# Turning double-precision weights into float32 on two engines, and spreading the recurrent units evenly, in an mLSTM + MLP kernel

## The chip, the cores and the metric

The kernel runs on one core of one Trainium2 chip. The metric is the device time of one execution in microseconds (us); lower is better. The engines of the core are named as in the profile: PE (TensorE, the matrix engine; PEld is its weight load), DVE (VectorE), ACT (ScalarE), POOL (GpSimd) and SP, whose queue issues nearly all DMAs.

## The reference

A recurrence over 768 positions for 4 x 8 heads of width 40 (an mLSTM with stabilised exponential gates), and behind it a two-layer MLP on its output, 3072 rows of 320, with a hidden width of 2048:

```python
for t in range(S):                       # per batch b and head h
    m_new = np.maximum(f_gate[:, :, t] + m, i_gate[:, :, t])
    f_stab = np.exp(f_gate[:, :, t] + m - m_new)
    i_stab = np.exp(i_gate[:, :, t] - m_new)
    C = f_stab * C + i_stab * outer(v_t, k_t)
    n = f_stab * n + i_stab * k_t
    y[:, :, t] = sigmoid(o_t) * (C @ q_t) / np.maximum(np.abs(n . q_t), 1.0)
x = y as (3072, 320)
h = x @ w_in                             # w_in  320 x 2048
out = (h * sigmoid(h)) @ w_out           # w_out 2048 x 320
```

The two weight matrices arrive as float64 (10.5 MB together); everything else is float32.

## The kernel before

**Units and steps.** The recurrence is cut into 12 chunks of 64 positions, and the batch into 2 pairs: 24 units of 128 output rows. Three units make a step, so there are 8 steps. For each step the MLP runs over 16 column blocks `fc` of the hidden width: `mm1(fc)` makes a 128 x 384 block `ph` (8 matmuls, weights and activations split in a high and a low part), ACT takes its tanh `th`, DVE makes the gated value `g` (step 0) or its high and low parts `gh`, `gl`, and `mm2(fc - 2)` adds that block's share to the three output tiles `pout`. In PE's order an `mm1` therefore alternates with an `mm2` two blocks behind. `ph` has two PSUM buffers, `pout` three, so the first `mm2` of a step waits until ACT has copied the step before it out of `pout` (tiles `ob`).

**Pieces.** The units of the *next* step are computed between the blocks of the running one. `piece` cuts a unit into five pieces. Piece 0 issues the loads of unit n+2, the scores of unit n+1 (`ps`), the values of unit n (`po`) and its state (`pu`): its front on PE. DVE then runs the chain `nq`, `den`, `x` that ends in the copy of line 433. Piece 1 transposes `x` on PE (`px`) into the step's activations `xh`, `xl`. Pieces 2 and 3 are gate activations and decays (`ko`, `lq`, `D`, on ACT and POOL). `SCHED` gives the unit reached at each step's start; the pieces of a step are spaced evenly between its two numbers, by the `while done < ...` loop. The numbers come to 3.2, 5, 3.4, 2.4, 2.4, 2.8 and 1.8 units in the seven steps.

**Weights.** The doubles come in 18 parts, each with one buffer `wr` out of ten: 8 parts of `w_in` (`i0` to `i7`, 512 doubles a partition, two column blocks each), 8 of `w_out` (`o0` to `o7`, 640 doubles) and two for the last 64 rows of `w_in` (`c0`, `c4`). `Part.make` turns the two 32-bit words of each double (`low`, `high`) into a float32 in `wt` (or `wo`), and then splits that into a high part (ACT copy, lines 224, 234 and 244) and a low part (DVE subtraction, lines 225, 235, 245). After each part the load of the next is issued. Five parts are made before step 0, the rest in step 0's blocks 0 to 5, by the digits of `FILL`.

**Order.** SP and, in the step loop, PE run in the order in which the code is written. DVE, ACT and POOL run in an order that the scheduler fixes when the program is built; each engine then executes its own list strictly in that order. A DVE instruction of a unit can thus stand behind weight instructions that have nothing to do with it.

Of the kernel before, what the change touches and what calls it, by code (L numbers as in the profile page):

```python
# [8 lines left out]
F32 = mybir.dt.float32  # L9
F32R = mybir.dt.float32r  # L10
U32 = mybir.dt.uint32
AF = mybir.ActivationFunctionType
ALU = mybir.AluOpType
PSUM = bass.MemoryType.PSUM
# [6 lines left out]
NU = NC * NP  # L21
# [3 lines left out]
UPS = 3  # L25
# [8 lines left out]
NBIG = 10  # L34
NWT = 3
PRI = 20
SCHED = [3, 6.2, 11.2, 14.6, 17.0, 19.4, 22.2, 24]
FILL = "2114231113212412"

TINY = 2.0**-15  # L40


@with_exitstack
def mlstm_mlp_kernel(
# [11 lines left out]
    nc = tc.nc  # L56
# [5 lines left out]
    pw = pool("pw", NWT)  # L62
# [15 lines left out]
        out=tri, in_=tri, compare_op=ALU.is_ge, fill=NEG, base=0,  # L78
# [10 lines left out]
    pq = pool("pq", DFF // 256)  # L89
    wo, wol = {}, {}  # L90
# [73 lines left out]
    WN = max(2 * WC, 2 * DM)  # L164
    wide = w_in.dtype != F32

    class Part:
# [7 lines left out]
        def load(self):  # L175
            K, nb, n, nm = self.K, self.nb, self.n, self.nm
            if wide:
                t = pb.tile([128, WN, 2], U32, tag="big", name=f"wr{nm}")[:, : nb * n, :]
                self.raw = t.rearrange("p (a f) w -> p a f w", a=nb)
                to, src = t.rearrange("p (a f) w -> p a (f w)", a=nb), self.src.bitcast(U32)  # L180
            else:
# [11 lines left out]
        def make(self):  # L193
            K, nb, n, nm = self.K, self.nb, self.n, self.nm
            full = self.raw
            if wide:


                low, high = full[:, :, :, 0], full[:, :, :, 1]
                bits = pw.tile([128, WN], U32, tag="wt", name=f"wt{nm}")  # L200
                bits = bits[:, : nb * n].rearrange("p (a f) -> p a f", a=nb)
                mag = full = bits.bitcast(F32)
                nc.scalar.activation(mag, high.bitcast(F32), AF.Abs)
                nc.vector.tensor_scalar(mag, mag, TINY, None, op0=ALU.max)
                nc.vector.tensor_scalar(
                    bits, bits, 3, 0x3FFFFFF8, op0=ALU.logical_shift_left, op1=ALU.bitwise_and
                )
                nc.vector.scalar_tensor_tensor(
                    out=bits, in0=high, scalar=0xC0000000, in1=bits,
                    op0=ALU.bitwise_and, op1=ALU.bitwise_or,  # L210
                )
                if self.i is not None:
                    full = wo[self.i] = pq.tile([128, nb, n], F32, tag="wo", name=f"w{nm}")
                nc.vector.scalar_tensor_tensor(  # L214
                    out=full.bitcast(U32), in0=low, scalar=29, in1=bits,
                    op0=ALU.logical_shift_right, op1=ALU.bitwise_or,
                )
            elif self.i is not None:
                wo[self.i] = pq.tile([128, nb, n], F32, tag="wo", name=f"w{nm}")
                nc.vector.tensor_copy(wo[self.i], full)  # L220
            if self.i is not None:
                return
            if K == 128:
                nc.scalar.copy(self.hi, full)
                nc.vector.tensor_tensor(
                    out=self.lo, in0=full, in1=self.hi.bitcast(F32), op=ALU.subtract
                )
            else:

                for k in range(2):  # L230
                    a, b = slice(k * K, (k + 1) * K), slice((1 - k) * K, (2 - k) * K)
                    cs = slice(k * n, (k + 1) * n)
                    hi = self.hi[a, :, cs]
                    nc.scalar.copy(hi, full[a])
                    nc.vector.tensor_tensor(
                        out=self.hi[b, :, cs], in0=full[a], in1=hi.bitcast(F32), op=ALU.subtract
                    )

    def split_out(i):

        full, hi = wo.pop(i), woh[:, 2 * i : 2 * i + 2, :]
        to, tag = (pq, "wo") if i else (pw, "wt")
        wol[i] = to.tile([128, 2, DM], F32R, tag=tag, name=f"wol{i}")
        nc.scalar.copy(hi, full)
        nc.vector.tensor_tensor(out=wol[i], in0=full, in1=hi.bitcast(F32), op=ALU.subtract)
# [25 lines left out]
    def wmake(n):  # L271

        for p in parts[nmade[0] : nmade[0] + n]:
            p.make()
            wload(1)
        nmade[0] = min(nmade[0] + n, len(parts))
# [16 lines left out]
    class Unit:  # L293
# [62 lines left out]
        def decay(self):  # L356
            nc.gpsimd.tensor_tensor(out=self.Dm, in0=self.Dm, in1=self.am, op=ALU.add)  # L357
            nc.scalar.activation(self.Dm, self.Dm, AF.Exp)

        def misc(self):  # L360
            nc.scalar.activation(self.ot, self.ot, AF.Tanh, scale=0.5)
            if self.c > 0:
                nc.scalar.activation(self.lq, self.lq, AF.Exp)  # L363
                self.qt = p2.tile([KS, H, L], F32, tag="qt", name=f"qt{self.n}")
                nc.gpsimd.tensor_tensor(out=self.qt, in0=self.q, in1=self.lq, op=ALU.mult)  # L365
# [109 lines left out]
    class Step:  # L475
# [10 lines left out]
        def mm1(self, fc):  # L486
# [14 lines left out]
            with tc.high_priority(offset=PRI):  # L501

                th = p2.tile([128, NT], F32, tag="th", name=f"th{j}_{fc}")
                nc.scalar.activation(th, ph, AF.Tanh, scale=0.5)  # L504
                if j == 0:
# [44 lines left out]
        def store(self, t):  # L550
# [4 lines left out]
            else:  # L555
                ob = pb.tile([128, DM], F32, tag="big", name=f"ob{n}")
            nc.scalar.activation(ob, self.po[t], AF.Copy, scale=0.5)  # L557
            for k in range(2):
# [4 lines left out]
    units = [Unit(n) for n in range(NU)]  # L563
    steps = {}

    def piece(i):

        n, k = divmod(i, 5)
        u = units[n]
        if k == 0:  # L570
            if n + 2 < NU:
                units[n + 2].load()
            if n + 1 < NU:
                units[n + 1].scores()
            u.values()
            u.state()
        elif k == 1:
            if n + 2 < NU:
                units[n + 2].shift()
            if n % UPS == 0:  # L580
                steps[n // UPS] = Step(n // UPS)
            u.xpose(steps[n // UPS])
        elif k == 2:
            if n + 1 < NU:
                units[n + 1].misc()
        elif k == 3:
            if n + 2 < NU:
                units[n + 2].decay()
# [57 lines left out]


    ctx.enter_context(tc.manual_schedule(engines={mybir.EngineType.PE}))
    done = 5 * UPS
    for j in range(NSTEP):  # L650
        st = steps[j]
        for fc in range(NFC):
            st.mm1(fc)
            wmake(int(FILL[fc]) if j == 0 else 2)
            if j == 1 and fc % 2 == 0:
                split_out(fc // 2)
            want = 5 * NU
            if j < NSTEP - 1:
                want = 5 * (SCHED[j] + (SCHED[j + 1] - SCHED[j]) * min(fc + 1, 15) / 15)
            while done < min(want, 5 * NU):  # L660
                piece(done)
                done += 1
            if fc >= LAG:
                st.mm2(fc - LAG)
            elif j > 0:
                steps[j - 1].mm2(NFC - LAG + fc)
# [71 lines left out]
```

## Time and profile before

| what | value |
|---|---|
| time, median of 3 runs | 543.53 us (539.04 to 546.12) |
| the profiled execution's own time | 542.31 us |
| its span in the trace | 540.4 us |
| PE busy / DVE busy / ACT busy / POOL busy | 446.9 / 331.6 / 196.6 / 133.2 us |
| mean granted TensorE clock | 0.94 |
| DMA moved | 48.5 MB |

The span is what the trace covers, from the first to the last instruction of the program; the 1.9 us between it and the profiled execution's own time lie around it. Busy times are sums over the whole span, which has two very different stretches: weights and first units up to about 150 us, the steady MLP after it. `L214` is line 214 of the kernel. In a row of the timeline stand start, duration, engine, line, operation, output<-inputs, and in brackets the idle time of the engine before it with what ended it.

### The profile page before, as it was taken

The numbers are of one execution on the slowest core, as the hardware profiler recorded it, in microseconds if no ns is written. First come the engines' busy times: TensorE is split into PE (matmuls) and PEld (weight loads), VectorE is DVE, ScalarE is ACT, GpSimd is POOL, SyncE is SP. The second block draws the span as 40 slices with busy tenths as digits, with TensorE's granted clock in tenths as the row PEclk, the third lists the DMA queues.
The fourth block names the chain that finished last, engine by engine and source line by source line (L and its number), as shares of the span: only waits on it lengthen the run. The fifth ranks groups of instructions, "written<-read, shape, count | busy, mean of one in ns | idle before, by whom it ended". The sixth has DMA issues, their size and how long they took to land.

```text
span 540.4 us, 10327 instructions
## 1 busy us (share of the span) xinstructions
PE 446.9 (83%) x4068; PEld 417.7 (77%) x4068; DVE 331.6 (61%) x669; ACT 196.6 (36%) x397; POOL 133.2 (25%) x129
## 2 busy tenths in 40 slices
PE   1532419269998998899999999899999999999995
PEld 0431318257888898898899998889989999999995
DVE  7999997945356676556656555366556453544441
ACT  1333334311243333533353243333534333334332
POOL 4644511502225443244124122141122000000000
PEclk9966658779999999999999999899999999999999
DMA  5999662512144334443124123230332001001001
GB/s 126 274 297 238 178 230 89 117 37 58 47 123 123 105 105 121 124 106 105 44 81 123 50 56 92 51 103 15 93 94 65 2 1 36 1 1 37 1 1 36
DMA packets 28163, 48.47 MB, mean 90 GB/s; under 512 B 4340, under 2 KB 15060, under 8 KB 28116
## 3 DMA queue, kind: packets, MB, share of 16 engines
q1 hardware_dynamic: 24228, 43.79, 29.7%
q10 hardware_dynamic: 3888, 4.03, 3.1%
q8 instruction: 32, 0.52, 0.4%
q14 instruction: 15, 0.12, 0.1%
HBM read 43.78 MB, written 4.03 MB: 88 GB/s over the span
## 4 chain that ended last, share of the span: by engine, by line
issue 29%; PE 23%; DMA 19%; DVE 13%; POOL 9%; SPq 4%; ACT 3%; ACTq 1%; POOLq 0%; DVEq 0%
PE ph L500 11%; PE pout L540 10%; DMA ko<-in_ko_dram 5%; DMA lq<-LFd 5%; POOL Cm L456 4%; DMA D<-LFd 4%; POOL D L357 3%; POOL am L349 2%; DMA qk<-in_qk_dram 2%; SPq L338 2%; DMA wri<-in_w_in_dram 1%; DVE wo L214 1%; SPq L304 1%; DVE D L393 1%; DVE Cm L462 1%
## 5 line engine op out<-in xcount | busy, mean ns | idle before, releaser
L500 PE MATMUL ph<-xh,wh 128*128 128x384 f32 x384 | 135.5, 353 | 1.0 <-ACT xh L470 1.0
L500 PE MATMUL ph<-xl,wh 128*128 128x384 f32 x384 | 132.1, 344 | 0.6 <-DVE xl L471 0.6
L513 DVE SCALAR_TENSOR_TENSOR th<-th,ph 128x384 f32<-128x384 f32 x112 | 61.9, 553 | 101.7 <-ACT th L504 101.7
L519 DVE TENSOR_TENSOR gl<-th,gh 128x384 fp32r<-128x384 f32 x112 | 77.2, 690 | 63.2 <-ACT gh L518 61.4
L540 PE MATMUL pout<-woh,gh 128*128 128x320 f32 x336 | 107.9, 321 | 5.6 <-ACT ob L557 5.3
L540 PE MATMUL pout<-woh,gl 128*128 128x320 f32 x336 | 104.0, 310 | 0.0
L540 PE MATMUL pout<-wol,gh 128*128 128x320 f32 x336 | 103.8, 309 | 0.0
L504 ACT ACTIVATE th<-ph 128x384 f32<-128x384 f32 x128 | 62.4, 487 | 98.9 <-PE ph L500 97.6
L500 PE MATMUL ph<-xh,wl 128*128 128x384 f32 x256 | 87.7, 343 | 0.0
L456 POOL TENSOR_TENSOR Cm<-Cm,lq 40x328 f32<-40x328 f32 x40 | 33.9, 847 | 176.1 <-PE po L408 158.0
L500 PEld LDWEIGHTS ph<-xh,wh 128*128 128x128 f32 x384 | 73.8, 192 | 2.6 <-ACT xh L470 1.3
L518 ACT CAST gh<-th 128x384 fp32r<-128x384 f32 x112 | 57.2, 511 | 50.2 <-DVE th L513 49.5
L500 PEld LDWEIGHTS ph<-xl,wh 128*128 128x128 f32 x384 | 73.7, 192 | 2.3 <-DVE xl L471 1.0
L540 PEld LDWEIGHTS pout<-woh,gh 128*128 128x128 f32 x336 | 63.2, 188 | 9.8 <-ACT ob L557 7.4
L540 PEld LDWEIGHTS pout<-woh,gl 128*128 128x128 f32 x336 | 63.3, 188 | 0.3 <-DVE gl L519 0.3
L540 PEld LDWEIGHTS pout<-wol,gh 128*128 128x128 f32 x336 | 63.3, 188 | 0.0
L468 PE MATMUL px<-ident,x 128*128 128x128 f32 x72 | 14.5, 307 | 50.7 <-DVE x L430 48.4
L468 PEld LDWEIGHTS px<-ident,x 128*128 128x128 f32 x72 | 8.6, 151 | 56.7 <-issue 33.4
L365 POOL TENSOR_TENSOR qt<-qk,lq 104x512 f32<-104x512 f32 x22 | 30.2, 1371 | 89.9 <-ACT lq L363 70.7
L500 PEld LDWEIGHTS ph<-xh,wl 128*128 128x128 f32 x256 | 49.2, 192 | 0.0
L363 ACT ACTIVATE lq<-lq 104x512 f32<-104x512 f32 x22 | 13.9, 630 | 79.6 <-DMA lq<-LFd 79.6
L357 POOL TENSOR_TENSOR D<-D,am 128x512 f32<-128x512 f32 x24 | 34.6, 1444 | 10.7 <-DMA D<-LFd 10.0
(74 smaller groups left out, 515.8 us busy)
## 6 DMA issues: line engine op xcount, KB each, us to landing
qk<-in_qk_dram SPq DMA_DIRECT2D x24, 416.0 KB
ko<-in_ko_dram SPq DMA_DIRECT2D x24, 320.0 KB
D<-LFd SPq DMA_DIRECT2D x48, 128.0 KB
wro<-in_w_out_dram SPq DMA_DIRECT2D x8, 640.0 KB
wri<-in_w_in_dram SPq DMA_DIRECT2D x8, 512.0 KB
vb<-in_vp_dram SPq DMA_DIRECT2D x48, 82.0 KB
out_dram<-ob ACTq DMA_DIRECT2D x48, 80.0 KB
lq<-LFd SPq DMA_DIRECT2D x22, 128.0 KB
```

Of the source, the lines that this page charges most:

```text
L338: nc.sync.dma_start(to[r], lf[k].unsqueeze(0).broadcast_to([w, 2, 4 * L]))
L357: nc.gpsimd.tensor_tensor(out=self.Dm, in0=self.Dm, in1=self.am, op=ALU.add)
L363: nc.scalar.activation(self.lq, self.lq, AF.Exp)
L365: nc.gpsimd.tensor_tensor(out=self.qt, in0=self.q, in1=self.lq, op=ALU.mult)
L456: nc.gpsimd.tensor_tensor(out=v, in0=v, in1=self.lq[r, :, L - 1].unsqueeze(2).broadcast_to([D, H, D1]), op=ALU.mult,)
L468: nc.tensor.transpose(px[:, c, :], self.x[:, c, :], ident)
L500: nc.tensor.matmul(ph, w, x, start=(i == 0), stop=(i == len(ops) - 1))
L504: nc.scalar.activation(th, ph, AF.Tanh, scale=0.5)
L513: nc.vector.scalar_tensor_tensor(out=th, in0=th, scalar=1.0, in1=ph, op0=ALU.add, op1=ALU.mult)
L518: nc.scalar.copy(gh, th)
L519: nc.vector.tensor_tensor(out=gl, in0=th, in1=gh.bitcast(F32), op=ALU.subtract)
L540: nc.tensor.matmul(self.po[t], g[:, ts], w, start=(fc == 0 and i == 0), stop=(last and i == len(ops) - 1),)
```

## The change

In `Part.make` five operations on each part become three. Before: ACT takes the magnitude of the high word (line 203); DVE clamps it (204), shifts and masks it (205), merges the sign (208), and merges the low word's top bits (214). Now ACT rescales the high word in place (`Prelu` with a tiny scale; its `alpha` serves the negative numbers), ACT turns the top byte of the low word into the three bits that are wanted, in place too, and one DVE operation shifts and merges both. In place means in `wr`, where the words of a double lie 8 bytes apart. A `w_out` part now goes to `wo` without passing `wt`.

The placing of units changes: `PLACES` gives, for step 0 and for all others, the block at which each of the next step's three units starts, and its pieces follow in the next blocks, one for each.

```diff
-SCHED = [3, 6.2, 11.2, 14.6, 17.0, 19.4, 22.2, 24]
+PLACES = ((3, 7, 11), (2, 7, 12))
...
-                bits = pw.tile([128, WN], U32, tag="wt", name=f"wt{nm}")
-                bits = bits[:, : nb * n].rearrange("p (a f) -> p a f", a=nb)
-                mag = full = bits.bitcast(F32)
-                nc.scalar.activation(mag, high.bitcast(F32), AF.Abs)
-                nc.vector.tensor_scalar(mag, mag, TINY, None, op0=ALU.max)
-                nc.vector.tensor_scalar(
-                    bits, bits, 3, 0x3FFFFFF8, op0=ALU.logical_shift_left, op1=ALU.bitwise_and
+                if self.i is not None:
+                    bits = pq.tile([128, nb, n], F32, tag="wo", name=f"w{nm}")
+                    wo[self.i] = bits
+                else:
+                    bits = pw.tile([128, WN], F32, tag="wt", name=f"wt{nm}")
+                    bits = bits[:, : nb * n].rearrange("p (a f) -> p a f", a=nb)
+                h32 = high.bitcast(F32)
+                nc.scalar.activation(h32, h32, AF.Prelu, scale=2.0**-112, alpha=-(2.0**32))
+                nc.scalar.activation(low, full.bitcast(U8)[:, :, :, 3], AF.Copy, scale=1 / 32, bias=-31 / 64)
+                nc.vector.scalar_tensor_tensor(
+                    out=bits.bitcast(U32), in0=high, scalar=3, in1=low,
+                    op0=ALU.logical_shift_left, op1=ALU.bitwise_or,
                 )
-                nc.vector.scalar_tensor_tensor(
-                    out=bits, in0=high, scalar=0xC0000000, in1=bits,
-                    op0=ALU.bitwise_and, op1=ALU.bitwise_or,
-                )
-                if self.i is not None:
-                    full = wo[self.i] = pq.tile([128, nb, n], F32, tag="wo", name=f"w{nm}")
-                nc.vector.scalar_tensor_tensor(
-                    out=full.bitcast(U32), in0=low, scalar=29, in1=bits,
-                    op0=ALU.logical_shift_right, op1=ALU.bitwise_or,
-                )
+                full = bits
...
             if j < NSTEP - 1:
-                want = 5 * (SCHED[j] + (SCHED[j + 1] - SCHED[j]) * min(fc + 1, 15) / 15)
-            while done < min(want, 5 * NU):
-                piece(done)
-                done += 1
+                for u, at in enumerate(PLACES[min(j, 1)]):
+                    if 0 <= fc - at < 4:
+                        piece((j + 1) * UPS + u, fc - at)
```

Three places of the engines' lists show what moves. In the rows stand the line, the operation, output<-inputs and the shape; the first number in a name is that of the unit, part or step (`wri7` is the raw buffer of part `i7`, `th0_4` the tanh of step 0, block 4), the number behind the underscore is that of the buffer.

The first place is SP's queue of loads in the middle of the weights, behind the loads of unit 4. Before:

```order
L186 DMA wri4_554<-in_w_in_dram 128x2x512
L186 DMA wro4_563<-in_w_out_dram 128x2x640
L304 DMA D5_565<-LFd_108 64x512 x2
L312 DMA qk5_568<-in_qk_dram 104x1024
L319 DMA ko5_570<-in_ko_dram 128x640
L325 DMA vb2_116<-in_vp_dram 64x328 x2
L338 DMA lq5_574<-LFd_108 64x2x256
L338 DMA lq5_574<-LFd_108 40x2x256
L186 DMA wri5_670<-in_w_in_dram 128x2x512
```

Now:

```order
L184 DMA wri4_540<-in_w_in_dram 128x2x512
L184 DMA wro4_546<-in_w_out_dram 128x2x640
L184 DMA wri5_567<-in_w_in_dram 128x2x512
L184 DMA wro5_586<-in_w_out_dram 128x2x640
L184 DMA wri6_615<-in_w_in_dram 128x2x512
L184 DMA wro6_623<-in_w_out_dram 128x2x640
L184 DMA wri7_629<-in_w_in_dram 128x2x512
L184 DMA wro7_637<-in_w_out_dram 128x2x640
L298 DMA D5_639<-LFd_108 64x512 x2
```

The loads of unit 5 moved from before part `i5` to behind all weights, because unit 3, whose piece 0 issues them, now starts at block 3 of step 0 and not at block 0.

The second place is ACT's list in the middle of step 0. Before, between the tanh of block 4 and that of block 5:

```order
L504 ACTIVATE th0_4_772<-ph0_4_763 128x384
L203 ACTIVATE wto6_881<-wro6_739 128x640
L203 ACTIVATE wti7_888<-wri7_748 128x512
L244 CAST woh_98<-wo5_781 128x640
L224 CAST wh_96<-wti6_783 128x2x256
L358 ACTIVATE D6_791<-D6_791 128x512
L361 ACTIVATE ko6_796<-ko6_796 128x320
L363 ACTIVATE lq6_800<-lq6_800 104x512
L203 ACTIVATE wto7_896<-wro7_758 128x640
L504 ACTIVATE th0_5_877<-ph0_5_868 128x384
```

Now, ahead of the tanh of block 4:

```order
L238 CAST woh_98<-wo4_625 128x640
L205 ACTIVATE wro5_586<-wro5_586 128x640
L206 ACTIVATE wro5_586<-wro5_586 128x640
L218 CAST wh_96<-wti5_631 128x2x256
L205 ACTIVATE wri6_615<-wri6_615 128x512
L206 ACTIVATE wri6_615<-wri6_615 128x512
L205 ACTIVATE wro6_623<-wro6_623 128x640
L206 ACTIVATE wro6_623<-wro6_623 128x640
L238 CAST woh_98<-wo5_729 128x640
L205 ACTIVATE wri7_629<-wri7_629 128x512
L206 ACTIVATE wri7_629<-wri7_629 128x512
L498 ACTIVATE th0_4_725<-ph0_4_716 128x384
```

Each part stands twice in ACT's list, and the conversion of `i7` stands one block earlier against the tanh values. One table load stands in ACT's whole list, as before.

The third place is DVE's list at the chain of a unit that PE transposes in the middle of step 0. Before, the end of unit 4's chain (its transposition stands in PE's list behind `mm1` of block 5):

```order
L422 RECIPROCAL den4_842<-den4_842 128x8
L225 TENSOR_TENSOR wl_97<-wti7_888,wh_96 128x2x256
L208 SCALAR_TENSOR_TENSOR wto7_896<-wro7_758,wto7_896 128x640
L427 TENSOR_TENSOR x4_848<-po4_825,den4_842 128x320
L214 SCALAR_TENSOR_TENSOR wo7_901<-wro7_758,wto7_896 128x640
L245 TENSOR_TENSOR wol1_1327<-wo1_493,woh_98 128x640
L430 SCALAR_TENSOR_TENSOR x4_848<-ko4_498,x4_848 128x320
L433 COPY x4_848<-x4_848 128x64
```

Now, the end of unit 3's chain (its transposition stands behind `mm1` of block 4):

```order
L416 RECIPROCAL den3_690<-den3_690 128x8
L219 TENSOR_TENSOR wl_97<-wti5_631,wh_96 128x2x256
L207 SCALAR_TENSOR_TENSOR wti6_733<-wri6_615 128x512
L421 TENSOR_TENSOR x3_696<-po3_673,den3_690 128x320
L207 SCALAR_TENSOR_TENSOR wo6_765<-wro6_623 128x640
L424 SCALAR_TENSOR_TENSOR x3_696<-ko3_445,x3_696 128x320
L207 SCALAR_TENSOR_TENSOR wti7_769<-wri7_629 128x512
L239 TENSOR_TENSOR wol0_1140<-wo0_358,woh_98 128x640
L427 COPY x3_696<-x3_696 128x64
```

The unit that is caught among the conversions is now unit 3 and not unit 4, and the last conversion ahead of its copy is that of `i7`. Over the whole program DVE has 54 instructions less and ACT 18 more. In PE's list of steps 1 to 6, pieces 0 now stand behind `mm1` of blocks 2, 7 and 12 and the transpositions behind `mm1` of blocks 3, 8 and 13. Before, steps 2 to 6 had an `mm1` of block 2 directly followed by the first `mm2` of the step; now a piece 0 stands between the two.

More of the change, by code (lines that the diff above doesn't have):

```diff
@@ L11 @@
 U32 = mybir.dt.uint32
+U8 = mybir.dt.uint8
 AF = mybir.ActivationFunctionType
@@ L36 @@
 PRI = 20
-SCHED = [3, 6.2, 11.2, 14.6, 17.0, 19.4, 22.2, 24]
+PLACES = ((3, 7, 11), (2, 7, 12))
 FILL = "2114231113212412"
-TINY = 2.0**-15
 @with_exitstack
@@ L564, in mlstm_mlp_kernel, with piece @@
     steps = {}
-    def piece(i):
-        n, k = divmod(i, 5)
+    def piece(n, k):
         u = units[n]
@@ L648, in mlstm_mlp_kernel @@
     ctx.enter_context(tc.manual_schedule(engines={mybir.EngineType.PE}))
-    done = 5 * UPS
     for j in range(NSTEP):
@@ L656, in mlstm_mlp_kernel @@
                 split_out(fc // 2)
-            want = 5 * NU
             if j < NSTEP - 1:
-                want = 5 * (SCHED[j] + (SCHED[j + 1] - SCHED[j]) * min(fc + 1, 15) / 15)
-            while done < min(want, 5 * NU):
-                piece(done)
-                done += 1
+                for u, at in enumerate(PLACES[min(j, 1)]):
+                    if 0 <= fc - at < 4:
+                        piece((j + 1) * UPS + u, fc - at)
             if fc >= LAG:
```

## The prediction

> **What bounds the kernel now.** I read the busy slices first, then the same in windows, then what PE waited for. Two slice rows of the page, each slice 13.5 us:
>
> ```profile
> PE   1532419269998998899999999899999999999995
> DVE  7999997945356676556656555366556453544441
> ```
>
> DVE is full for the first seven slices and PE is not; from the ninth it is the other way round. The windows (length, busy time and number of instructions of each engine, granted clock, DMA share, GB/s) fix the places:
>
> ```profile
> core 0: us, PE busy (x) PEld busy (x) DVE busy (x) ACT busy (x) POOL busy (x), PEclk, DMA share, GB/s
> 20.00:40.00 20.00, 10.51 (x153) 9.12 (x155) 19.79 (x42) 8.17 (x14) 9.76 (x8) 0.76 1.00 303
> 40.00:60.00 20.00, 4.66 (x71) 3.22 (x67) 19.81 (x37) 7.72 (x15) 7.62 (x5) 0.59 1.01 254
> 60.00:65.00 5.00, 4.40 (x48) 3.50 (x50) 5.00 (x6) 2.58 (x6) 3.52 (x3) 0.55 0.53 132
> 80.00:98.00 18.00, 17.00 (x140) 14.98 (x141) 13.42 (x25) 7.92 (x14) 4.44 (x4) 0.86 0.43 115
> 98.00:112.00 14.00, 0.46 (x3) 0.14 (x1) 13.90 (x24) 4.75 (x8) 3.85 (x3) 0.64 0.24 56
> 112.00:152.00 40.00, 38.92 (x310) 32.24 (x311) 18.89 (x42) 7.53 (x16) 6.51 (x7) 0.95 0.21 57
> ```
>
> In these stretches up to 112 us DVE is 99% busy, but for 80 to 98 (75%); ACT is at 34 to 52%, and DMA is full only until about 62 us. The list of waits and PE's timeline name the wait that ends last there:
>
> ```profile
> PE px L468 <- DVE x L430: 48.4, 18, 13.9
> PEld pout L540 <- ACT ob L557: 7.4, 7, 2.4
> ...
> 57.20 0.66 PE L468 MATMUL px<-ident,x 128*128 128x128 f32 x2 [12.02 <-DVE x L430]
> 112.39 0.88 PE L468 MATMUL px<-ident,x 128*128 128x128 f32 x3 [13.94 <-DVE x L430]
> 115.73 0.58 PE L500 MATMUL ph<-xh,wh 128*128 128x384 f32 x1
> 152.45 0.58 PE L500 MATMUL ph<-xh,wh 128*128 128x384 f32 x1
> ```
>
> PE stood 13.94 us before unit 4's transposition, because its `x` on DVE stood among weight conversions. From there to step 1 (152.45) PE is full: 40.1 us. After that the span is PE's, 540.4 - 152.45 = 387.9 us with the tail. Unit 2's transposition, the last before step 0, had waited 12.02 in the same way. So the change can win before 112 us on DVE, and later only in PE's small waits.
>
> **What the edit of the weights removes.** Three views by line, the whole span, busy us and number of instructions (lines 204, 205, 208), then ACT's groups (count, busy us, mean ns):
>
> ```profile
> 0.00:541.00 541.00, 10.50 (x18) 0.94 0.33 90
> 0.00:541.00 541.00, 13.03 (x18) 0.94 0.33 90
> 0.00:541.00 541.00, 16.01 (x18) 0.94 0.33 90
> ...
> L203 ACT ACTIVATE wto<-wro 128x640 f32<-128x640 f32 x8 | 6.3, 783 | 2.1 <-DMA wro<-in_w_out_dram 2.1
> L203 ACT ACTIVATE wti<-wri 128x512 f32<-128x512 f32 x8 | 5.4, 671 | 1.8 <-DMA wri<-in_w_in_dram 1.8
> L244 ACT CAST woh<-wo 128x640 fp32r<-128x640 f32 x8 | 5.8, 721 | 17.6 <-DVE wo L214 17.6
> L224 ACT CAST wh<-wti 128x512 fp32r<-128x512 f32 x8 | 4.9, 617 | 9.8 <-DVE wti L214 9.8
> L504 ACT ACTIVATE th<-ph 128x384 f32<-128x384 f32 x128 | 62.4, 487 | 98.9 <-PE ph L500 97.6
> L214 DVE SCALAR_TENSOR_TENSOR wti<-wri,wti 128x512 uint32<-128x512 uint32 x8 | 5.4, 680 | 0.0
> L214 DVE SCALAR_TENSOR_TENSOR wo<-wro,wto 128x640 uint32<-128x640 uint32 x8 | 9.5, 1189 | 0.0
> ```
>
> DVE loses 10.5 + 13.0 + 16.0 = 39.5 us, 2.2 us a part, all before 112 us. Line 214 is replaced by one operation of the same kind; no row has both inputs 8 bytes apart. I take 0.68 and 0.82 us (what line 214 takes when nothing disturbs it); the upper end is the row's 1.19 us. ACT gains 18 operations, and all 36 work in place, which no row shows. From below they cost a plain copy, 0.62 and 0.72 us; from above I take POOL's 1.44 us for a 128x512 tile, the slowest elementwise row near. The nearest row is line 203, which reads the same words: 0.67 and 0.78 us. I take that.
>
> The writes 8 bytes apart have a rule in the Trainium skill, "SBUF — State Buffer", the note on cachelines: lines are 16 bytes, and two hits in each suffice for full bandwidth. Words 8 bytes apart hit each line twice, so by it the in-place operations cost nothing extra. For reads the trace agrees (671 ns against 617 for contiguous data); no run here shows the writes.
>
> **What is late next: ACT's list and DMA.** With DVE relieved, unit 3 is the one whose chain stands among conversions; its copy stands behind part `i7`, whose two ACT operations stand at the end of an unbroken row of conversions. When can they be done? DMA rows of SP's queue, and one load on the chain that ended last:
>
> ```profile
> 49.00 1.18 SPq L338 DMA_DIRECT2D lq<-LFd  x2
> 57.88 1.12 SPq L325 DMA_DIRECT2D vb<-in_vp_dram  x2
> 68.36 1.21 SPq L338 DMA_DIRECT2D lq<-LFd  x2
> 77.16 0.37 SPq L186 DMA_DIRECT2D wri<-in_w_in_dram  x1
> ...
> 26.64 4.31 DMA lq<-LFd
> ```
>
> Before, SP sat from 59.0 (57.88 + 1.12) to 68.36 on unit 5's `lq` load (its buffer was held by unit 3), and `i7` was issued only at 77.16. That load now stands behind the weights. DMA was full to about 62.6 us (0.53 of the window 60 to 65), with unit 5's D, qk, ko and vb in it: 256 + 416 + 320 + 164 KB, 4.7 us at 254 GB/s. Without them everything to `o4` is in at 58, and `i5`, `o5`, `i6`, `o6`, `i7` (3 x 512 + 2 x 640 KB, 2.9 MB) take 11.4 us more: `i7` lands at **69**.
>
> ACT: unit 4's `lq` was issued at 49.0 to 50.2; with the 4.3 us of an `lq` load, and something more in a full queue, it lands near 56. Behind it, up to `i7`'s second operation, stand 8 in-place operations of 512 (5.4 us), 6 of 640 (4.7), one `lq` exponential (0.63), three tanh (1.5), four casts of `wh` (2.5) and two of `woh` (1.4): 16.1 us, so 72.1, later than DMA. Then DVE: merge 0.68, one `wol` 0.83, the copy 0.2, and some 1.2 us of hand-overs: unit 3's transposition at **75 us**. Is PE there by then? Unit 2's transposition was at 57.2; seven parts ahead of it at 2.2 us less would give 42. DMA is as full as before, so I take 48. Five `mm1`, two `mm2` and a front, two of the blocks at half clock, are some 16 us by the prices below: PE is done at 64, stands 11 us, and its clock falls as before.
>
> The Trainium skill, "ScalarE: Activation LUTs", speaks against the move: its "Rules for kernel authors" put multiplications on VectorE, as faster. Here the rows are even (671 ns on ACT, 680 on DVE), and what counts is the list that is shorter. By the formula in "What ACT_TABLE_LOAD costs" (186 ns + 0.833 ns an element) the 14 operations are an estimated 9.2 us, not 10.1; the transposition would come 0.9 us earlier.
>
> **From there to step 1.** Prices of PE, from starts of `mm1` in step 0, then in step 3:
>
> ```profile
> 124.77 0.57 PE L500 MATMUL ph<-xh,wh 128*128 128x384 f32 x1
> 130.45 0.58 PE L500 MATMUL ph<-xh,wh 128*128 128x384 f32 x1
> 134.68 0.58 PE L500 MATMUL ph<-xh,wh 128*128 128x384 f32 x1
> 149.44 0.58 PE L500 MATMUL ph<-xh,wh 128*128 128x384 f32 x1
> ...
> 278.08 0.34 PE L500 MATMUL ph<-xh,wh 128*128 128x384 f32 x1
> 280.80 0.34 PE L500 MATMUL ph<-xh,wh 128*128 128x384 f32 x1
> 286.21 0.33 PE L500 MATMUL ph<-xh,wh 128*128 128x384 f32 x1
> 288.56 0.52 PE L468 MATMUL px<-ident,x 128*128 128x128 f32 x3 [0.79 <-DVE x L430]
> 290.23 0.33 PE L500 MATMUL ph<-xh,wh 128*128 128x384 f32 x1
> 486.90 0.34 PE L500 MATMUL ph<-xh,wh 128*128 128x384 f32 x1
> ```
>
> Step 0: a block 3.01 (149.44 to 152.45), with a front 5.68, with a transposition 4.23. From unit 3's transposition remain: its block at half clock, 3.34 (112.39 to 115.73); blocks 5 to 15, 11 x 3.01 = 33.1; two fronts, 2 x 2.67; two transpositions, 2 x 1.22. That is 44.2: step 1 at 75 + 44.2 = **119.2**.
>
> **The even spread.** Later a block takes 2.72 (278.08 to 280.80), with a front 5.41 (+2.69), with a transposition that waits 0.79 for DVE 4.02 (+1.30). Six steps of three units: 6 x (43.5 + 8.1 + 3.9) = 333.0. The last step and tail stay: 540.4 - 486.9 = 53.5. I take 3 off because units 22 and 23 have no state and less scores and `Cm` work. Sum 383.5, against 387.9 before, although unit 6's front (2.7) moves in from step 0 and every transposition now waits 0.79 (before, five units had it across a step's end and did not). What pays is the 7.4 us of waits on `ob`: each step from 1 to 6 now has a front between block 2 and the first `mm2`, which covers them, as in steps 1 and 3 before; one remains. The bounds: without that cover the waits come back, 7 us more; less than the sum it cannot be by much, since steps 1 to 6 are then PE's own time and its 0.79.
>
> Span 119.2 + 383.5 = 502.7, with 1.9 around it 504.6; the profiled execution (542.31) lay 1.2 under the median, so **506 us**.
>
> **Rivals.**
> - PE is not held at all: ACT overlaps its operations and all lands early, the transposition comes at 64 and the clock stays (1.5 saved): 12.5 less, **493**. For it: DVE's count alone allows it. Against: `i7` does not land before 69, and its merge stands ahead of the copy.
> - In-place operations are dear: at 1.44 us each the 14 ahead of unit 3's copy cost 10.1 more: **516**; with the `ob` waits kept **523**. For it: no row shows such a write; against it: line 203 reads the same words at little extra. The VectorE rule of "ScalarE: Activation LUTs" in the Trainium skill would then be borne out.
> - The freed time is eaten by another wait. Against the nearest one, unit 5's loads, now behind all weights: they can be in by 78, and unit 5's values stand at block 11, near 105. To stay within 2% the transposition would have to come after 102 us: **533 to 554**.
> - Slower: the in-place pair blocks ACT's list. From 0.72 us, each operation would have to take over 4.1 us (14 x 3.4 = 48 us, transposition at 123) to pass 554: **560**. The largest ACT mean of this size in the trace is 0.78, so this has little for it.
>
> **How the numbers follow.** Forecast (500 to 512) 0.64, PE not held 0.12, dear operations 0.17, another wait 0.05, slower 0.02. The range, 491 to 525, takes both ends of the unknown prices. About 2% (11 us) is what a measurement of this kernel tells from no change: faster 0.93, same 0.05, slower 0.02.
>
> **What would show it.** In the changed profile: step 1 starts near 119 and not at 152; DVE is no longer full between 40 and 112; unit 3's transposition at 70 to 80 after a wait of about 11 us; in-place rows near 0.67 and 0.78 us; waits on `ob` under 2 us; 18 transposition waits of 0.79. It is wrong if the ACT rows are above 1 us, if `i7` is issued after 70, or if steps 1 to 6 exceed 57 us.

## The result and the profile after

The changed kernel takes **507.55 us** (median of 4 runs, 506.51 to 508.46) against 542.97 us (4 runs, 539.04 to 546.12): ratio 0.935, 95% interval 0.929 to 0.942. The profiled execution took 506.51 us with a span of 504.7 us.

Lines of `Part.make` and `Unit` have moved. The new operations are 205 (`Prelu`), 206 (low word) and 207 (merge); `px` is line 462, its `x` on DVE 424, the copy of its last 64 columns 427, `ph` 494, `pout` 534, `ob` 551. First the busy slices of the page (each 12.6 us), then the windows with the columns explained in the prediction:

```profile
PE   1444769999999999999999999999999989999994
DVE  6688596553564665674576566665656465453331
```

```profile
40.00:60.00 20.00, 9.81 (x67) 8.05 (x64) 12.40 (x20) 10.62 (x20) 7.38 (x6) 0.71 1.00 246
60.00:70.00 10.00, 10.00 (x111) 8.22 (x110) 9.39 (x19) 9.95 (x18) 2.32 (x3) 0.91 1.05 357
70.00:80.00 10.00, 4.63 (x15) 3.13 (x15) 9.95 (x15) 8.52 (x16) 3.47 (x3) 0.66 0.91 204
80.00:98.00 18.00, 17.31 (x150) 14.29 (x150) 9.49 (x20) 3.97 (x9) 7.61 (x8) 1.00 0.32 92
120.00:152.00 32.00, 30.49 (x307) 28.01 (x306) 18.52 (x42) 11.23 (x24) 7.30 (x7) 1.00 0.26 71
```

DVE is no longer full from 40 to 112 us: 62% from 40 to 60, full only from 60 to 80, half empty after that. ACT and DMA are now full with it from 60 to 70. From 80 us on PE is full, not from 112. PE's waits, and rows of its timeline with the starts of steps 1, 2 and 7 as the last three:

```profile
PE px L462 <- DVE x L424: 19.2, 21, 2.6
PE ph L494 <- DVE g L502: 3.2, 1, 3.2
PE pout L534 <- ACT ob L551: 0.6, 1, 0.6
...
58.20 0.51 PE L494 MATMUL ph<-xh,wh 128*128 128x384 f32 x1 [3.18 <-DVE g L502]
69.82 0.34 PE L494 MATMUL ph<-xl,wh 128*128 128x384 f32 x1
72.81 0.66 PE L462 MATMUL px<-ident,x 128*128 128x128 f32 x2 [2.65 <-DVE x L424]
76.19 0.48 PE L462 MATMUL px<-ident,x 128*128 128x128 f32 x1 [2.72 <-DVE x L427]
120.00 0.58 PE L494 MATMUL ph<-xh,wh 128*128 128x384 f32 x1
176.31 0.34 PE L494 MATMUL ph<-xh,wh 128*128 128x384 f32 x1
451.20 0.34 PE L494 MATMUL ph<-xh,wh 128*128 128x384 f32 x1
```

Unit 3's transposition at 72.8 to 76.7 is the longest wait left behind the first 17 us: 5.4 us in two parts. Ahead of it block 0 still waits 3.4 us for `xh` (at 48.4) and block 2 3.2 us for `g`. Step 1 starts at 120.0 (152.45 before): 32.5 of the 35.7 us by which the span fell. Steps 1 to 6 take 331.2 us, and the rest 53.5. The prices of the new operations, from the groups by line and shape (count, busy us, mean ns):

```profile
L205 ACT ACTIVATE wro<-wro 128x640 f32<-128x640 f32 x8 | 6.4, 799 | 1.7 <-DMA wro<-in_w_out_dram 1.6
L206 ACT ACTIVATE wro<-wro 128x640 uint32<-128x640 uint8 x8 | 6.3, 782 | 0.0
L205 ACT ACTIVATE wri<-wri 128x512 f32<-128x512 f32 x8 | 5.4, 679 | 2.8 <-DMA wri<-in_w_in_dram 2.8
L206 ACT ACTIVATE wri<-wri 128x512 uint32<-128x512 uint8 x8 | 5.3, 668 | 0.0
L207 DVE SCALAR_TENSOR_TENSOR wo<-wro 128x640 uint32<-128x640 uint32 x8 | 7.6, 953 | 2.0 <-ACT wro L206 2.0
L207 DVE SCALAR_TENSOR_TENSOR wti<-wri 128x512 uint32<-128x512 uint32 x8 | 6.1, 762 | 2.4 <-ACT wri L206 2.4
```

And the place that decides step 0: the start of ACT's row of conversions behind unit 4's `lq`, its end (part `i7`), and what DVE and POOL do there.

```profile
58.59 0.63 ACT L357 ACTIVATE lq<-lq 104x512 f32<-104x512 f32 x1 [1.46 <-DMA lq<-LFd]
...
71.41 0.67 ACT L205 ACTIVATE wri<-wri 128x512 f32<-128x512 f32 x1
71.98 0.66 ACT L206 ACTIVATE wri<-wri 128x512 uint32<-128x512 uint8 x1
...
72.17 0.49 DVE L424 SCALAR_TENSOR_TENSOR x<-ko,x 128x320 f32<-128x320 f32 x1
72.68 0.69 DVE L207 SCALAR_TENSOR_TENSOR wti<-wri 128x512 uint32<-128x512 uint32 x1
73.29 1.90 DVE L239 TENSOR_TENSOR wol<-wo,woh 128x640 fp32r<-128x640 f32 x1
75.11 1.03 DVE L427 COPY x<-x 128x64 f32<-128x64 f32 x1
...
72.85 1.65 POOL L351 TENSOR_TENSOR D<-D,am 128x512 f32<-128x512 f32 x1 [5.12 <-DMA D<-LFd]
74.58 1.50 POOL L343 TENSOR_TENSOR am<-mask,aT 128x512 f32<-128x512 f32 x1
```

Unit 3's copy stands behind `i7`'s merge and one `wol`. ACT hands `i7` over at 72.64, and DVE is free at 72.66: both lists arrive at the same moment.

### The profile page after: what moved, and what is told of

Its sections match the earlier page's. It is cut to its first block, busy times and chain, and to the rows that moved or that the text cites. A ratio compares the mean times of both kernels' runs of the same rounds, so it can differ in the third digit from the quotient of the medians.

```text
span 504.7 us, 10288 instructions
## 1 busy us (share of the span) xinstructions
PE 444.0 (88%) x4068; PEld 415.2 (82%) x4068; DVE 295.4 (59%) x615; ACT 206.1 (41%) x415; POOL 129.0 (26%) x129
## 4 chain that ended last, share of the span: by engine, by line
issue 28%; PE 25%; DMA 20%; POOL 12%; DVE 5%; SPq 5%; ACT 4%; ACTq 1%; POOLq 0%
PE pout L534 12%; PE ph L494 11%; DMA D<-LFd 9%; DMA lq<-LFd 6%; POOL Cm L450 5%; POOL D L351 4%; DMA ko<-in_ko_dram 3%; POOL am L343 3%; SPq L332 3%; DMA out_dram<-ob 1%; SPq L298 1%; PE po L402 1%; ACT ob L551 1%; DMA wrc<-in_w_in_dram 1%; ACT th L498 1%
## 5 line engine op out<-in xcount | busy, mean ns | idle before, releaser
L513 DVE TENSOR_TENSOR gl<-th,gh 128x384 fp32r<-128x384 f32 x112 | 75.9, 677 | 62.3 <-ACT gh L512 59.2
L359 POOL TENSOR_TENSOR qt<-qk,lq 104x512 f32<-104x512 f32 x22 | 28.5, 1297 | 81.0 <-ACT lq L357 75.4
L351 POOL TENSOR_TENSOR D<-D,am 128x512 f32<-128x512 f32 x24 | 32.5, 1356 | 24.0 <-DMA D<-LFd 23.6
```

The source lines that it names most:

```text
L513: nc.vector.tensor_tensor(out=gl, in0=th, in1=gh.bitcast(F32), op=ALU.subtract)
```

## The experiments

Each kernel ran on one chip with the kernel before; the ratios are to that. A difference to the changed kernel in us is one between chips, on which the kernel before took 542.0 to 544.2 us. A span is that of the profiled execution.

### One half of the change at a time

**Only the conversion**, with the units where they stood before:

```diff
-PLACES = ((3, 7, 11), (2, 7, 12))        # of the changed kernel
+SCHED = [3, 6.2, 11.2, 14.6, 17.0, 19.4, 22.2, 24]
```

> The kernel before with only the new conversion of the weights; the pieces of the units stand where they stood before. Theory (the two parts of the change add): in step 0 PE does what it did before, with unit 3's chain at block 0 and unit 4's transposition at block 5, but the seven conversions ahead of the x copies cost DVE 2.2 us less each; step 1 starts at 115 to 124 us (152.4 before, 120.0 with the whole change), and from there to the end 386 to 388 us pass as in the kernel before (387.9) because the waits on ob come back: span 503 to 511, time 505 to 513 us. Rival (most of the gain is the place of unit 5's loads, which here stand ahead of i5 again, so that SP stands on unit 5's lq until about 68 us and i7 is issued near 77): step 1 at 127 to 135, time 517 to 525 us.

Measured: 525.5 us, ratio 0.966 (0.961 to 0.971). The time behind step 1 is 525.1 - 136.2 = 388.9 us, 0.9 above the theory's range. Step 1 is 16 us later than with the whole change, at 136.2, just past the rival's 127 to 135. But the rival's reason is not the cause: moving unit 5's loads gives this kernel nothing (below). Its rows on PE, then on ACT:

```profile
71.02 0.88 PE L465 MATMUL px<-ident,x 128*128 128x128 f32 x3 [9.74 <-DVE x L427]
96.14 0.87 PE L465 MATMUL px<-ident,x 128*128 128x128 f32 x3 [7.89 <-DVE x L427]
136.24 0.58 PE L497 MATMUL ph<-xh,wh 128*128 128x384 f32 x1
...
71.93 0.48 ACT L467 CAST xh<-px 128x384 fp32r<-128x384 f32 x1 [0.93 <-PE px L465]
74.49 0.49 ACT L501 ACTIVATE th<-ph 128x384 f32<-128x384 f32 x1 [2.08 <-PE ph L497]
74.88 0.67 ACT L208 ACTIVATE wri<-wri 128x512 f32<-128x512 f32 x1
```

Two transpositions are held, not one. Unit 3's stands at block 0 and waits 9.74 us for an `x` behind conversions. ACT, whose list goes on with that unit's `xh` and a tanh, takes up the weights (`i5`) again only at 74.88. Then unit 4's, at block 5, waits 7.89 behind the rest of the conversions.

**Only the places**, with the old conversion:

```diff
-                nc.scalar.activation(h32, h32, AF.Prelu, ...)     # and the two lines behind it
+                nc.scalar.activation(mag, high.bitcast(F32), AF.Abs)
+                ...                                                # the four VectorE operations
```

> The whole change but for the conversion of the weights, which is the old one (one ScalarE and four VectorE operations). Theory: DVE is full from 20 to 110 us as before and unit 3's or unit 4's transposition waits for conversions on it; step 1 starts at 148 to 156, and behind it 384 to 386 us as in the changed kernel: span 533 to 541, time 535 to 543 us, 0.99 to 1.00 of before. Rival (moving unit 5's loads behind the weights is what wins, since i7 comes 19 us sooner): step 1 at 130 to 142, time 517 to 530 us. In both, the waits of PEld on ob fall from 7.4 to under 1.5 us.

Measured: 525.6 us, ratio 0.967 (0.963 to 0.971): the rival's numbers. The kernel before, then this one:

```profile
79.94 0.87 PE L468 MATMUL px<-ident,x 128*128 128x128 f32 x3 [6.53 <-DVE x L430]
...
91.98 0.66 PE L467 MATMUL px<-ident,x 128*128 128x128 f32 x2 [12.50 <-DVE x L429]
139.11 0.58 PE L499 MATMUL ph<-xh,wh 128*128 128x384 f32 x1
```

DVE is no less full than it was (busy for 17.9 of the 18 us from 80 to 98, for 13.4 before), but it holds PE for long only once in step 0, at 92 us. Before, unit 3's transposition stood ahead of block 1 and came at 79.94, and unit 4's came at 112.39. With unit 3 behind block 3, PE does the first blocks while the conversions run. Step 1 comes 13.3 us earlier, and the waits on `ob` go (7.4 to 0.8 us). The places take unit 5's loads with them, behind the weights; what share of the gain is theirs is not separated here. Putting them back costs 5.9 us in the changed kernel (below).

So the two halves are worth the same, -17.3 and -17.2 us, and together 35.4: within the intervals they add.

**The conversion, and the places in step 0 alone:**

```diff
+                if j == 0:                       # units 3, 4, 5 behind blocks 3, 7, 11
+                    ...
+            while j and done < min(want, 5 * NU):   # from step 1 on the old table
+                piece(*divmod(done, 5))
```

> The new conversion, and the even spread in step 0 alone: there units 3, 4 and 5 stand behind blocks 3, 7 and 11, and from step 1 on the pieces come by the old table (from unit 6 at the start of step 1). It lies between the kernel with only the new conversion (525.5 us) and the changed kernel (507.6). Theory (what the kernel with only the conversion lacks is the places in step 0, where two transpositions, of units 3 and 4, stand among conversions and not one): step 1 at 119 to 121 us as in the changed kernel, behind it 388 to 391 us by the old table and with unit 6's front in it: 509 to 514 us. Rival (the lateness comes from the table of the later steps as much as from step 0): 517 to 523 us.

Measured: 521.0 us, ratio 0.956 (0.948 to 0.963). Step 1 starts at 121.4, near the theory's 119 to 121, so the places in step 0, with the loads that move with them, are indeed what the kernel with only the conversion lacks. But behind it lie 400.7 us, not 388 to 391, and the time falls into the rival's range.

```profile
129.36 0.87 PE L463 MATMUL px<-ident,x 128*128 128x128 f32 x3 [3.71 <-DVE x L425]
...
PEld pout L535 <- ACT ob L552: 8.7, 6, 3.0
```

With the old table unit 6's front and transposition come right at the start of step 1, PE waits 3.71 us for it and runs that stretch at a lower clock (0.95 from 121.4 to 196.4, where the changed kernel has 1.00 from 120 to 195), and the `ob` waits are back. The table of the later steps does not fit the new step 0; spreading them is worth some 11 us there by the ratios (13.5 by the times on two chips), not the 4.4 of the sum.

### Unit 5's loads

In the changed kernel they are put back ahead of `i5`; in the kernel with only the conversion they are moved behind the weights:

```diff
             wmake(int(FILL[fc]) if j == 0 else 2)
+            if j == fc == 0:
+                units[5].load()
```

> The changed kernel with the loads of unit 5 issued where they stood before the change, behind o4 and ahead of i5, and nothing else moved. Theory (SP stands on unit 5's lq, whose buffer unit 3 holds, and the loads take 4.7 us of a full DMA): i7 is issued at 64 to 70 us and no longer at 58.4, and lands 5 to 10 us later; unit 3's transposition and step 1 come 5 to 10 us later: 512 to 518 us. Rival (the place of these loads costs nothing, because unit 3's lq is free by then and the weights have to wait for their turn on ScalarE anyway): under 2 us more, 507 to 509.5 us.

```diff
-            if n + 2 < NU:
+            if n == 3:
+                units[5].load_d()                # its qk, ko, vb and lq in unit 4's piece 0
+            elif n + 2 < NU:
```

> The kernel with only the new conversion (525.5 us), and the loads of unit 5's qk, ko, vb and lq moved from ahead of i5 to behind the weights; only its D is loaded where it was. The pieces of the units stand where they stood before the change. Theory A (in that kernel the late step 1, 136.2 instead of 120.0, comes from SP and DMA, which bring i5 to i7 late): 5 to 10 us come back: 515 to 521 us. Theory B (it comes from the places of the pieces: unit 3's transposition stands at block 0, ScalarE waits with the conversions of i5 to i7 behind its xh copy and the tanh of block 0, and unit 4's x copy stands behind all of them on VectorE): under 3 us come back, 522.5 to 526 us.

Measured: 513.4 us (0.948; 0.944 to 0.953), 5.9 us more than the changed kernel and in the theory's range, with step 1 7.1 us later; and 525.4 us (0.969; 0.963 to 0.974), no change, as theory B has it. The first does not go the theory's way: `i7` is issued at 72.1 and not at 64 to 70, and unit 3's transposition comes no later (71.9). It slips through ahead of the late weights, and unit 4's is held:

```profile
98.45 0.87 PE L462 MATMUL px<-ident,x 128*128 128x128 f32 x3 [7.82 <-DVE x L424]
...
90.05 1.32 PE L440 MATMUL pu<-vb,kw 128*40 128x82 f32 x16 [5.77 <-DVE D L390]
```

In the second (the last row) PE is held at unit 4's front, by DVE's `D`, instead of its transposition; step 1 starts 2.4 us sooner (133.9), and the time behind it is 2.5 us longer (391.4). In these two kernels SP's order thus pays only where the pieces let it.

### What sets unit 3's transposition

**One more ACT operation a part**, and **each merge done twice on DVE**:

```diff
+                nc.scalar.activation(h32, h32, AF.Copy)           # e5: between 205 and 206
```

> The changed kernel with one more ScalarE operation for each weight part: a plain copy of the high words onto themselves, in place, between the two new operations. It changes no value. Theory (ScalarE's list, 99% busy from 60 to 70 us, sets when unit 3's transposition can start): the five to seven parts from c4 to i7 that stand in an unbroken row cost 0.67 to 0.78 us each, the transposition comes 3.5 to 5 us later and step 1 with it, at 123 to 126: 510.5 to 513.5 us. Rival (the landing of the weights, DMA being full until 70 us, or VectorE behind it sets the time, and ScalarE has slack between landings): under 1.5 us more, 507 to 509 us.

```diff
+                nc.vector.scalar_tensor_tensor(out=bits.bitcast(U32), ...)   # e6: line 207 again
```

> The changed kernel with the merge of each weight part done twice on VectorE (the second writes the same words again). It changes no value. Theory (VectorE has slack behind ScalarE's list until the last part): only the merges of the last one or two parts ahead of unit 3's copy count, 0.7 to 1.5 us, and the ones of the earlier parts lie in VectorE's idle time: 508 to 510 us. Rival (VectorE is as full as ScalarE from 60 to 75 us, so each merge of the five parts from i5 to i7 counts): 3.5 to 5 us more, 511 to 513 us.

Measured: 509.0 us (0.940; 0.935 to 0.946), 1.4 more, which the intervals do not tell from nothing; and 519.4 us (0.958; 0.953 to 0.963), 11.8 more. Both lie outside the theory's ranges; the first is at the upper edge of its rival's, the second above its rival's too. But neither is a clean price, because DVE's list came out in another order. Unit 3's copy and the merges in DVE's timeline, first with the ACT operation (two merges between them left out), then with the double merge:

```profile
74.83 0.92 DVE L428 COPY x<-x 128x64 f32<-128x64 f32 x1
...
79.80 0.69 DVE L208 SCALAR_TENSOR_TENSOR wti<-wri 128x512 uint32<-128x512 uint32 x1
```

```profile
84.94 0.81 DVE L211 SCALAR_TENSOR_TENSOR wo<-wro 128x640 uint32<-128x640 uint32 x1
88.40 0.20 DVE L431 COPY x<-x 128x64 f32<-128x64 f32 x1
```

With the ACT operation `i7` is merged at 79.80, 7.1 us later than the 72.68 of the changed kernel: the conversions did get slower. But the copy now stands ahead of the merges of `i6`, `o6` and `i7`, and the transposition, from 74.94 to 76.3, ends no later than before (76.7). With the double merge the copy stands behind all eighteen parts, and the transposition waits 12.1 us. As far as these two runs tell, what counts is **how many conversions stand ahead of unit 3's copy on DVE**, more than what each takes.

**The copy alone, on another engine.** This edit leaves the rest of DVE's list around it as it was:

```diff
-            nc.vector.tensor_copy(xf[:, DM : DM + 64], xf[:, DM - 64 : DM])
+            (nc.gpsimd if n == 3 else nc.vector).tensor_copy(xf[:, DM : DM + 64], xf[:, DM - 64 : DM])
```

> The changed kernel with one instruction moved to another engine: the last operation of unit 3's x, the copy of 64 columns, runs on GpSimd and no longer on VectorE, where it stood behind the merge of i7 and one wol. Theory (what holds PE at 73.5 to 76.2 us is only that place in VectorE's list): the copy is done near 73.3, the wait of 2.72 goes, and step 1 comes 2 to 3 us earlier, or up to 4 if PE's clock no longer drops: 503.5 to 505.5 us. Rival (PE's wait is paid by the conversions as such: the tanh and casts that follow on ScalarE, and blocks 4 and 5 then wait instead): under 1 us, 506.5 to 508 us.

```profile
73.19 0.66 POOL L427 COPY x<-x 128x64 f32<-128x64 f32 x1 [5.07 <-DVE x L424]
...
73.20 1.18 PE L462 MATMUL px<-ident,x 128*128 128x128 f32 x3 [2.83 <-DVE x L424]
```

Measured: 505.1 us (6 runs; 0.928, 0.925 to 0.931), 2.4 less than the changed kernel and within the theory's range, though the two intervals still touch. All three transposes run at 73.2, and the second wait of 2.72 is gone. Step 1 starts at 118.84, only 1.2 us earlier where the theory had 2 to 3: the matmuls behind still ran at a low clock (0.62 from 73 to 81 us), and block 5 became 1.0 us longer.

### The waits of 0.79, and the cover of the `ob` waits

**The transposition two blocks behind the front:**

```diff
-                        piece((j + 1) * UPS + u, fc - at)
+                        piece((j + 1) * UPS + u, (0, 2, 1, 3)[fc - at])
```

> The changed kernel with one edit: the transposition of a unit stands two blocks behind its front and no longer one (the piece that prepares the next unit's misc operands changes places with it). Theory (18 transpositions wait 0.79 us each for DVE's x, because only one block of PE work lies between front and transposition): these waits go, 16 to 18 x 0.79 = 12.6 to 14.2 us, and nothing takes their place: 491 to 496 us. Rival 1 (the DVE chain to x is set by something that moves along, the state or the am of the next unit): the wait stays, 505 to 510 us. Rival 2 (the misc piece, now one block sooner, delays x on DVE or ACT and a new wait comes up): 498 to 505 us.

Measured: **486.6 us**, ratio 0.8955 (0.891 to 0.900): 21 us less than the changed kernel, more than the theory's 12.6 to 14.2. Transpositions of step 3, in the changed kernel and here:

```profile
280.23 0.52 PE L462 MATMUL px<-ident,x 128*128 128x128 f32 x3 [0.78 <-DVE x L424]
...
272.24 0.49 PE L462 MATMUL px<-ident,x 128*128 128x128 f32 x3
```

No transposition waits from step 1 on. Each now adds 0.33 us to its block (3.05 against 2.72) where it added 1.30: the wait of 0.79 was not the whole price, some 0.2 us more went with it, for a reason that no row shows. That is 2.9 in a full step; for the 16 transpositions of steps 1 to 6 that waited (those of units 22 and 23 did not) it is 15.5, and these steps take 315.7 us instead of 331.2. Step 1 also starts 2.4 us earlier (117.65). The two profiles thus differ by 17.8 us; what is left of the 21 lies between executions.

**The front one block later,** behind the first `mm2`:

```diff
-PLACES = ((3, 7, 11), (2, 7, 12))
+PLACES = ((3, 7, 11), (3, 7, 12))
```

> The changed kernel with one number moved: in steps 1 to 6 the first unit's front stands behind block 3 and no longer behind block 2, that is behind the first mm2 of the step and no longer ahead of it. Theory (the front ahead of the first mm2 is what covers the wait for ob): the waits of PEld and PE on ob come back to 0.8 to 2.5 us a step, 5 to 15 us in all: 511 to 521 us. Rival (the waits went because each step now holds three units, whatever their block): no change, 505 to 509 us.

```profile
PEld pout L534 <- ACT ob L551: 7.3, 7, 2.2
```

Measured: 513.1 us (0.944; 0.939 to 0.949), 5.5 more, as the theory has it: it is the front ahead of the first `mm2` that covers `ob`.

**Going further.** The transposition two blocks behind the front, and unit 3 two blocks later as well; and the same with unit 3's copy on POOL instead:

```diff
-PLACES = ((3, 7, 11), (2, 7, 12))
+PLACES = ((5, 9, 12), (2, 7, 12))
```

> The kernel with the transposition two blocks behind the front (486.6 us), and in step 0 the fronts of units 3, 4 and 5 stand behind blocks 5, 9 and 12 and no longer 3, 7 and 11. Theory (in step 0 PE waits for x because unit 3's chain stands among the conversions on VectorE; two more blocks of mm1 ahead of it cover that): step 1 comes 1.5 to 4 us earlier, 482.5 to 485 us. Rival (VectorE takes unit 3's chain behind all merges then, and the wait for x comes back there, or blocks 4 to 6 wait for their own weights): 486 to 490 us.

```profile
85.95 0.20 DVE L427 COPY x<-x 128x64 f32<-128x64 f32 x1
...
86.06 0.88 PE L462 MATMUL px<-ident,x 128*128 128x128 f32 x3 [5.78 <-DVE x L424]
```

> The kernel with the transposition two blocks behind the front (486.6 us), and unit 3's copy of 64 columns on GpSimd as well. There PE waited 0.62 and 1.79 us for unit 3's x. Theory: the second of these waits goes, and the low clock behind it: 484 to 486 us. Rival (no change, since the tanh of the blocks behind it waits for ScalarE's conversions): 486 to 488 us.

Measured: 494.2 us (0.909; 0.906 to 0.913), worse than without it by more than the rival thought: unit 3's copy now stands behind every merge on DVE and comes at 85.95, so the two blocks of cover are eaten and PE waits 5.78 us. And 486.2 us (0.895; 0.892 to 0.899), as the rival has it: the same as without the copy on POOL, although its profile starts step 1 at 115.5 and not at 117.65. The version with the transposition two blocks behind the front beats both kernels by one reordered line.

## Why the prediction was right, point by point

- **The total:** 506 predicted, 507.55 measured; span 502.7 against 504.7.
- **What bounds the kernel:** right. PE stood behind an `x` among conversions, and with the conversion alone unit 4's wait fell from 13.94 to 7.89 us. One thing was passed over: unit 3's transposition was held as well before (6.53 us at 79.94).
- **Prices of the new operations:** taken 0.67 and 0.78 us on ACT, 0.68 and 0.82 on DVE. Measured 0.67 to 0.68 and 0.78 to 0.80 on ACT. On DVE 0.76 and 0.95 as means, 0.69 and 0.82 where nothing disturbs them. By the note on cachelines of the Trainium skill's "SBUF — State Buffer" words 8 bytes apart should cost nothing extra. For the writes the trace agrees: 668 to 679 ns in place, where line 203 with the same reads took 671 before. For the reads the prediction said so too readily: 671 against 617 for contiguous data is 9% more. By the formula of the Trainium skill's "ScalarE: Activation LUTs", section "What ACT_TABLE_LOAD costs", the in-place operations are an estimated 612 and 719 ns; the measurement decides.
- **ACT's list as what is late next:** `i7` through ACT predicted at 72.1, measured at 72.64. That these are so close is luck: unit 4's `lq` came at 58.59 and not near 56, and the row behind it took 14.05 us and not 16.1, because ACT starts each operation some 0.1 us before the last one ends (71.98 against 71.41 + 0.67), and the sum added whole durations. Behind `lq` ACT waits for no DMA; when `i7` landed (69 by the sum, at 254 GB/s) no row shows, and DMA moved 357 GB/s from 60 to 70. And it was not ACT alone: DVE was free only at 72.66. Which of the two would be late without the other stays open, since the experiments meant to tell changed DVE's order.
- **Unit 3's transposition at 75:** two thirds of it came at 72.81 and the last at 76.19. The prices behind ACT were off: `wol` taken at 0.83 took 1.90, the copy at 0.2 took 1.03, and of the 1.2 us of hand-overs next to nothing was seen. From ACT's end to the last third were 3.55 us against 2.9: again two errors that mostly cancel.
- **"PE is done at 64, stands 11 us":** this term was wrong in size. PE was done at 70.16 (69.82 + 0.34) and stood 5.4 us. Unit 2's transposition came at 44.6, sooner than the 48 taken, but from there PE needed 25.5 us for what was priced at 16. It had stood earlier: 3.4 us for `xh` before block 0, 3.18 us at 55 for `g`, since ACT's tanh stands behind part `c4`, which ACT waited for until 55.2, and more in the blocks behind it. The blocks were priced by PE alone. The error did no harm, because the transposition's time, set by ACT and DVE, does not depend on it.
- **From there to step 1, 44.2:** measured 43.8 (76.19 to 120.00).
- **The even spread:** steps 1 to 6 330.0 predicted (333.0 less 3), 331.2 measured; the rest 53.5 and 53.5; `ob` waits down to one. Right, with the waits near 0.79 as foreseen, though 16 of them and not 18. The gain behind step 1 is 3.2 us (387.9 to 384.7) and not 4.4: the 7.4 us on `ob` are those of the weight loads, and PE's own matmuls waited 5.3 for it before, in steps 2, 4, 5, 6 and 7. Step 3 too had a front behind block 2 before (that of unit 15), as the prediction has it; the section on the change, which leaves out that front, is wrong there.
- **What the sum hid:** it gives step 0's whole gain to the conversion and only 4.4 us to the places. Alone, the conversion gave half. The sum came out all the same, as it followed unit 3's chain in the changed order, with both edits in it.

Of the rivals, none came: PE was held, the in-place operations were not dear, and no later wait took the gain.

## What to carry to other kernels

When a tensor that another engine waits for is made on a busy engine, count what stands ahead of it in that engine's own list, and ask which work the waiting engine could do meanwhile: moving the waiter was worth as much here as halving the load. An extra operation can reorder such a list, so read the list of every experiment before calling its time a price. And a wait of 0.79 us that recurs 16 times, taken in the sum as the cost of the plan, was with what hung on it 15.5 of some 21 us, for one reordered line.

## What the hardware showed that was not expected

In this trace DVE's merges and subtractions of weights, which read two SBUF tiles, wait until a POOL operation that is already running has ended. The merge of a 640 part takes 0.82 us where POOL is idle; the one at 51.02 took 1.88:

```profile
51.02 1.88 DVE L207 SCALAR_TENSOR_TENSOR wo<-wro 128x640 uint32<-128x640 uint32 x1 [1.23 <-ACT wro L206]
...
50.95 1.28 POOL L351 TENSOR_TENSOR D<-D,am 128x512 f32<-128x512 f32 x1 [2.17 <-DMA D<-LFd]
```

POOL began 0.07 us sooner and ended at 52.23; 0.67 us later the merge was done. Around unit 3's copy, in the rows quoted with the result, it is the same: `i7`'s merge began ahead of POOL's `D` (72.68 against 72.85) and took its normal 0.69; `wol` began behind it and ended 0.69 after it; the copy, with one input, ended 0.06 after POOL's `am`. Of the weight operations on DVE that overlap one on POOL, the four that began first kept their time (0.68 to 0.82 us), and the seven that began second were all longer (0.85 to 1.90), each ending 0.55 us (512 elements) or 0.68 (640) after POOL. The Trainium skill, "SBUF — State Buffer", section "Who interferes with whom", calls the two engines' common pair of ports an exclusive lock that the first to issue holds to its end. These rows agree; some 1.9 us of it (1.90 for 0.82 and 1.03 for 0.2) stood in the chain that the prediction priced without it.
